# Every third stretch of values made on the chip by GpSimd instead of loaded, in a fused window attention and mixture-of-experts kernel

## The chip, the cores and the metric

The kernel runs on one core of a Trainium2 chip. The metric is the device time of one execution in microseconds (us), lower is better. Engines are called PE (TensorE), DVE (VectorE), ACT (ScalarE), POOL (GpSimd) and SP (SyncE, which issues most of the DMAs here).

## What is computed

There are 8 batches of 8 heads, 512 local and 32 global positions, and a head dimension of 64. Local queries see the global keys and a window of 32 positions to either side; global queries see everything. The result, 4352 tokens of 512 features, goes through a mixture of 8 experts where each token is sent to the one expert with the highest logit.

```python
k_all = concat([k_g, k_l]); v_all = concat([v_g, v_l])
out_g = softmax(q_g @ k_all.T / 8) @ v_all
s_ll = where(abs(pos_i - pos_j) <= 32, q_l @ k_l.T / 8, -1e9)
out_l = softmax(concat([q_l @ k_g.T / 8, s_ll])) @ concat([v_g, v_l])
x = concat([out_g, out_l])                      # 4352 tokens x 512
e = argmax(normed(x) @ normed(expert_emb).T / tau)
out = gate * (relu(x @ w1[e]) @ w2[e])
```

## The kernel before

The work has two stages. The attention stage goes over 8 batches in 4 steps each, 32 steps in all, with 34 slots of program: in slot g the scores of step g are made, the probabilities of step g-1 are turned, and the values of step g-2 are multiplied (the table that `at` fills, lines 843 to 859, and `slot`, line 954). After that the expert stage works on 128-token items with matrix products of 512 columns.

A step treats 4 blocks of 32 queries for 8 heads. Each block of queries needs 128 rows of keys and values: three neighbouring blocks of 32 local rows and the 32 global rows. On the host the values are laid out as 14 such stretches for each batch (`va`, the loop at line 1331): stretch s holds the local blocks s, s+1, s+2, with the global rows in the last place where s is 0, 3, 6, ..., one place earlier where s is 1, 4, ..., and two places earlier where s is 2, 5, .... So stretch 2 reads b2, g, b3, b4 from top to bottom, stretch 0 reads b0, b1, b2, g, and stretch 3 reads b3, b4, b5, g. A stretch is 128 partitions by 260 numbers for each of two groups of heads.

`load_v` (line 290) loads the stretches of one step, 3 or 4 of them by `VCUT` (line 54), for each group: pairs of 260 KB and single ones of 130 KB. `vals` (line 302) says where a stretch stands. `values` (line 529) multiplies them, 64 small matrix products a step. `g_values` (line 616) uses stretches 0, 3, 6, 9, 12 and 13 of a batch for the global queries.

All loads go through SP's queue in the order in which `later` (line 930) lists them for each slot. `deal` and `tick` hand them out evenly over six places in PE's work of that slot, and `paced` (line 262) makes each wait for the PE instruction at that place. Up to 8 loads of this queue are under way at once. The finished token rows leave by indirect DMAs that POOL issues (`send`, line 792; 32 for the local rows), one in each slot from 9 to 28 right after the scores, two in slots 29 and 30.

Of the kernel before, what the change touches and what calls it, by code (L numbers as in the profile page):

```python
# [12 lines left out]
F32 = mybir.dt.float32  # L13
# [12 lines left out]
D = 64  # L26
# [7 lines left out]
P = 128  # L34
# [11 lines left out]
NWIN = NBQ - 2  # L46
VH = D + 1
# [3 lines left out]

GAP = 2
RS = RW + 16
VCUT = (0, 3, 7, 11, NWIN)
VP = 528
VS = 2 * VP
NV = 6
WRUN = 1024
WS = WRUN + GAP

# [13 lines left out]
def _mask_of(i):  # L74
    return 3 if i == 0 else 4 if i == NBQ - 1 else (i - 1) % 3
# [25 lines left out]
def tile_kernel(ctx: ExitStack, tc: tile.TileContext, qk, va, emb, tau, wraw, cst, out):  # L101
    nc = tc.nc
    NB = qk.shape[0]
# [121 lines left out]
    with ExitStack() as actx:  # L225
# [2 lines left out]
        gapi.tile([P, 8], F32, name="gapi_")  # L228
        io = actx.enter_context(tc.tile_pool(name="io", bufs=2))
        vio = actx.enter_context(tc.tile_pool(name="vio", bufs=NV))  # L230
        rt = actx.enter_context(tc.tile_pool(name="rt", bufs=2))
        sp = actx.enter_context(tc.tile_pool(name="sp", bufs=4))
        sm = actx.enter_context(tc.tile_pool(name="sm", bufs=4))
# [9 lines left out]
        NSTEP = 4 * NB  # L243
# [3 lines left out]
        state = {}  # L247
# [4 lines left out]
        def after(ins, mark):  # L252

            tc.add_manual_dep(
                ins.ins,
                mark.ins.name,
                mybir.DependencyInfo(mybir.DependencyClass.Sync, mybir.DependencyReason.DATA),
                reason="pace",
            )
            return ins  # L260

        def paced(ins):

            return after(ins, state["mark"]) if "mark" in state else ins
# [22 lines left out]
            lo, hi = k * RW // 2, (k + 1) * RW // 2  # L287
            paced(nc.sync.dma_start(state["raw", b][:, j, lo:hi], qk[b, :, j * RW + lo : j * RW + hi]))

        def load_v(g, n, m=2):  # L290

            b, s = divmod(g, 4)
            nw = VCUT[s + 1] - VCUT[s]
            if ("v", g) not in state:
                state["v", g] = vio.tile([P, 2, VS], F32, name="vt")
            grp, w = n % 2, n // 2 * m
            for a in range(w, min(w + m, nw), 2):
                n = (min(a + 2, nw) - a) * 4 * VH
                c, to = (VCUT[s] + a) * 4 * VH, a // 2 * VP
                paced(nc.sync.dma_start(state["v", g][:, grp, to : to + n], va[b, grp, :, c : c + n]))  # L300

        def vals(b, w, grp, j):

            s = next(s for s in range(4) if w < VCUT[s + 1])
            n = w - VCUT[s]
            c = n // 2 * VP + (n % 2 * 4 + j) * VH
            return state["v", 4 * b + s][:, grp, c : c + VH]


        first = io.tile([P, 4, RS], F32, name="raw")  # L310
# [10 lines left out]
        def first_step(s):  # L321
            first_part(s * P, (s + 1) * P if s < 3 else QW)
            first_part(QW + KCUT[s] * BQ, QW + KCUT[s + 1] * BQ)
# [3 lines left out]
        for n, i in enumerate((0, NBQ - 2)):  # L327
            for q in range(4):
                m = _mask_of(i + q % 2) * P
                rows = slice(32 * q, 32 * q + 32)  # L330
                nc.gpsimd.tensor_copy(twins[rows, n], mask[rows, m : m + P])
        first_step(1)
        load_v(0, 0, 4)
        load_v(0, 1, 4)
        first_step(2)

        def setup_loads():
# [191 lines left out]
        def values(g):  # L529

            b, s = divmod(g, 4)
            state["o", g] = po = ps_o.tile([P, 2, 512], F32, name="po")
            for grp in range(2):
                pT = state["pT", g, grp]
                for j in range(4):
                    for k in range(4):
                        ins = nc.tensor.matmul(  # L537
                            po[32 * k : 32 * k + 32, grp, j * VH : (j + 1) * VH],
                            pT[:, col(s, k, j) : col(s, k, j) + 32],
                            vals(b, _window(4 * s + k), grp, j),  # L540
                            start=True,
                            stop=True,
                        )
                tick(ins, 4 + grp)
            state["valued"] = ins
# [70 lines left out]
        def g_values(b, grp):  # L616

            og = bank()
            for c, (w, kn) in enumerate(((0, 96), (3, 96), (6, 96), (9, 96), (12, P), (13, P))):
                for j in range(4):  # L620
                    rows = slice(32 * j, 32 * j + 32)
                    nc.tensor.matmul(  # L622
                        og[rows, :VH],
                        gT[:kn, grp, c, rows],
                        vals(b, w, grp, j)[:kn],
                        start=(c == 0),
                        stop=(c == 5),
                    )
            rg = sm.tile([P, 1], F32, name="rg")
            nc.vector.tensor_scalar(rg, og[:, D:VH], 1e-9, None, op0=ALU.add)  # L630
            nc.vector.reciprocal(rg, rg)
            on = sp.tile([P, D], F32, name="on", bufs=2)
            nc.vector.tensor_scalar(on, og[:, :D], rg, None, op0=ALU.mult)
            r0 = 32 * (b % 4)
            xg = state["xg", b // 4][r0 : r0 + 32, 0, grp * 4 * D : (grp + 1) * 4 * D]
            for j in range(4):
                nc.gpsimd.tensor_copy(xg[:, j * D : (j + 1) * D], on[32 * j : 32 * j + 32])
# [191 lines left out]
        for b in range(3, NB - 1, 4):  # L829
            a = b // 4  # L830
# [12 lines left out]
        def at(g, phase, f, *args):  # L843
            plan.setdefault((g, phase), []).append(lambda: f(*args))


        SCORE, TURN, MAX, ACT, VALUE, LOGIT, TAKE, ACT2, GVAL, NORM, BACK, SMALL, LATE, GLOB, SEND = range(15)

        for g in range(NSTEP):
            b, s = divmod(g, 4)  # L850
            at(g, SCORE, scores, g)
            for grp in range(2):
                at(g + 1, TURN, turned, g, grp)
            for grp in range(2):
                at(g, MAX, maxima, g, grp)
                at(g, ACT2 if grp else ACT, exps, g, grp)
                at(g + 1, ACT, take, g, grp)
            at(g + 2, VALUE, values, g)
            at(g + 2, NORM, normed, g)

        for b in range(NB):
            g0 = 4 * b + (0 if b else 2)
# [3 lines left out]
            for part in range(3):  # L866
                g = 4 * b + (2 + part // 2 if b else 4)
# [62 lines left out]
        def later(g, f, *args):  # L930
            loads[g].append(lambda: f(*args))

        for g in range(1, NSTEP):
            for n in range(4):
                later(min(g, NSTEP - 2), load_v, g, n)
        for b in range(1, NB):
            for j in range(4):
                for k in range(2):
                    later(max(4 * b - 5 + j, 0), load, b, j, k)
        for n in range(EARLY + 2):  # L940
            later(4 + n, first_fill, n)

# [6 lines left out]
        for g in loads:  # L949
            n = len(loads[g])  # L950
# [441 lines left out]
```

## Time and profile before

| | us |
|---|---|
| median of 3 runs (lowest, highest) | 726.94 (724.56, 732.45) |
| the profiled execution | 725.47 |
| its span, first to last instruction | 723.6 |

The span ends 1.9 us short of the time of the same execution. Nearly one third of the span is the attention stage, the rest the expert stage. "Idle before, releaser" in a row says how long the engine had nothing to run just before that instruction, and what ended it; "issue" as a releaser means that no semaphore and no other engine is seen to have held it up.

### The profile page before, as it was taken

How to read it: one execution, taken by the hardware profiler on the slowest of the kernel's cores; microseconds unless marked ns; L12 is line 12 of the kernel's file. 1: busy time of each engine (PE TensorE's matmuls, PEld its weight loads, DVE VectorE, ACT ScalarE, POOL GpSimd, SP SyncE). 2: the span in 40 equal slices, each digit the busy share in tenths (PEclk: the TensorE clock that was granted, in tenths of full speed). 3: DMA queues.
4: the chain of work that ended last, by engine and by line, in shares of the span. 5: the costliest groups of instructions: out<-in, count | busy, mean ns of one | idle time of the engine just before them, and what ended most of it. 6: DMA issues, size and time to landing. Idle time of an engine off the chain costs nothing.

```text
span 723.6 us, 23361 instructions
## 1 busy us (share of the span) xinstructions
PE 674.1 (93%) x7867; PEld 535.3 (74%) x7869; DVE 422.2 (58%) x1449; ACT 458.6 (63%) x956; POOL 273.0 (38%) x318
## 2 busy tenths in 40 slices
PE   9888878878878998999999999999999999999996
PEld 4666666656756546888888888888888888888885
DVE  2778777888677763545554554545455545455443
ACT  4776767747767365656565666666666656565664
POOL 2011222222212344545454545444454545454543
PEclk9999999999899999999999999999999999999999
DMA  8988989878997257746565665656565746575654
GB/s 274 351 249 258 256 236 279 285 213 292 283 301 227 77 214 267 260 165 249 186 232 205 209 225 193 244 185 248 169 249 179 259 157 240 185 231 206 223 210 156
DMA packets 66588, 165.13 MB, mean 228 GB/s; under 512 B 6548, under 2 KB 14868, under 8 KB 66464
## 3 DMA queue, kind: packets, MB, share of 16 engines
q1 hardware_dynamic: 60704, 145.67, 60.5%
q0 software_dynamic: 5760, 17.87, 7.0%
q8 instruction: 71, 1.16, 0.7%
q14 instruction: 53, 0.43, 0.2%
HBM read 142.49 MB, written 22.07 MB: 227 GB/s over the span
## 4 chain that ended last, share of the span: by engine, by line
PE 88%; issue 5%; DMA 2%; DVE 2%; SPq 1%; ACT 1%; POOL 0%; DVEq 0%; POOLq 0%
PE g L1198 18%; PE g L1199 18%; PE g L1203 18%; PE po L537 5%; PE hps L1221 4%; PE pt L514 4%; PE s_ps L467 4%; PE pt L654 2%; PE xps L1174 2%; PE pt L622 2%; DMA raw<-in_qk_dram 2%; PE po L355 2%; PE pt L574 1%; PE pt L681 1%; PE s_ps L456 1%
## 5 line engine op out<-in xcount | busy, mean ns | idle before, releaser
L1194 DVE TENSOR_TENSOR WL<-stg,WH 128x512 f32 (+1 forms) x144 | 150.5, 1045 | 130.2 <-ACT WH L1192 130.2
L1194 POOL TENSOR_TENSOR WL<-stg,WH 128x512 f32 (+1 forms) x144 | 174.3, 1210 | 88.9 <-ACT WH L1192 87.9
L1192 ACT CAST WH<-stg 128x512 f32 (+1 forms) x288 | 177.4, 618 | 9.2 <-DMA stg<-in_wraw_dram 4.6
L1198 PE MATMUL g<-WH,hH 128*128 (+1 forms) x288 | 119.5, 415 | 0.0
L1198 PE MATMUL g<-WH,xH 128*128 (+1 forms) x288 | 116.0, 403 | 0.0
L1199 PE MATMUL g<-WL,hH 128*128 (+1 forms) x288 | 113.3, 393 | 0.0
L1203 PE MATMUL g<-WH,xL 128*128 (+1 forms) x288 | 112.6, 391 | 0.0
L1199 PE MATMUL g<-WL,xH 128*128 (+1 forms) x288 | 112.5, 390 | 0.0
L147 POOL DMA_INDIRECT out_dram<-ob x37 | 37.2, 1006 | 151.7 <-ACT ob L145 142.4
L507 ACT ACTIVATE pb<-pb,nm 128x128 f32<-128x128 f32 x256 | 80.1, 396 | 11.7 <-DVE nm L490 11.5
L1203 PE MATMUL g<-WH,hL 128*128 (+1 forms) x288 | 83.4, 391 | 0.0
L1224 DVE TENSOR_TENSOR hL<-hps,hH 128x512 fp32r<-128x512 f32 x72 | 49.8, 692 | 53.8 <-ACT hH L1223 53.6
L1203 PEld LDWEIGHTS g<-WH,hL 128*128 128x128 f32 x288 | 54.1, 188 | 12.1
L1203 PEld LDWEIGHTS g<-WH,xL 128*128 128x128 f32 x288 | 54.1, 188 | 11.6
L145 ACT ACTIVATE ob<-g,xr 128x512 f32<-128x512 f32 x36 | 24.8, 688 | 59.5 <-PE g L1203 59.5
L1199 PEld LDWEIGHTS g<-WL,xH 128*128 128x128 f32 x288 | 54.2, 188 | 10.2 <-DVE ob L146 0.2
L1198 PEld LDWEIGHTS g<-WH,xH 128*128 128x128 f32 x288 | 54.2, 188 | 10.2 <-issue 0.2
L1198 PEld LDWEIGHTS g<-WH,hH 128*128 128x128 f32 x288 | 54.4, 189 | 9.5
L1199 PEld LDWEIGHTS g<-WL,hH 128*128 128x128 f32 x288 | 54.4, 189 | 9.1
L1215 ACT ACTIVATE h<-g 128x512 f32<-128x512 f32 x72 | 42.9, 595 | 28.8 <-PE g L1203 28.8
L794 POOL DMA_INDIRECT xs<-xt,si x32 | 32.1, 1004 | 75.9 <-PE pt L514 27.5
L1223 ACT CAST hH<-hps 128x512 fp32r<-128x512 f32 x72 | 42.0, 584 | 24.6 <-PE hps L1221 24.6
(200 smaller groups left out, 985.4 us busy)
## 6 DMA issues: line engine op xcount, KB each, us to landing
stg<-in_wraw_dram SPq DMA_DIRECT2D x36, 2048.0 KB, 9.8
vt<-in_va_dram SPq DMA_DIRECT2D x96, 260.0 KB, 4.7
raw<-in_qk_dram SPq DMA_DIRECT2D x56, 304.0 KB, 5.1
xr<-xs SPq DMA_DIRECT2D x38, 257.0 KB, 2.7
vt<-in_va_dram SPq DMA_DIRECT2D x32, 130.0 KB, 5.1
stg<-in_wraw_dram SPq DMA_DIRECT2D x16, 256.0 KB, 5.5
xs<-fill SPq DMA_DIRECT2D x12, 257.0 KB, 3.0
stg<-in_wraw_dram SPq DMA_DIRECT2D x4, 512.0 KB, 7.1
```

Of the source, the lines that this page charges most:

```text
L147: nc.gpsimd.indirect_dma_start(out=out[:, :], out_offset=bass.IndirectOffsetOnAxis(ap=ob[:, DM : DM + 1].bitcast(U32), axis=0), in_=ob[:, ...
L507: nc.scalar.activation(pb[:, cs], pb[:, cs], AF.Exp, bias=nm[:, n : n + 1], scale=-1.0)
L537: ins = nc.tensor.matmul(po[32 * k : 32 * k + 32, grp, j * VH : (j + 1) * VH], pT[:, col(s, k, j) : col(s, k, j) + 32], vals(b, _window(4 ...
L794: ins = nc.gpsimd.indirect_dma_start(out=xs[:, :], out_offset=bass.IndirectOffsetOnAxis(ap=st["si"][:, t : t + 1], axis=0), in_=get(t), in ...
L1192: made.append(nc.scalar.copy(WH[:, ds(ra, 1), cs], s3))
L1194: made.append(eng.tensor_tensor(WL[:, ds(r, 1), cs], s3, WH[:, ds(r, 1), cs], ALU.subtract))
L1198: reads.append(nc.tensor.matmul(o.unsqueeze(1), a, WH2[:, ds(rp, 1), sl], start=first, stop=False))
L1199: reads.append(nc.tensor.matmul(o.unsqueeze(1), a, WL2[:, ds(rp, 1), sl], start=False, stop=False))
L1203: reads.append(nc.tensor.matmul(o.unsqueeze(1), a, WH2[:, ds(rp, 1), sl], start=False, stop=last))
L1215: nc.scalar.activation(h[:, nh * 512 : (nh + 1) * 512], g, AF.Relu)
L1223: nc.scalar.copy(hv, hp_)
L1224: nc.vector.tensor_tensor(hL[:, nh * 4 : nh * 4 + 4, :].rearrange("p c n -> p (c n)"), hp_, hv, ALU.subtract)
```

## The change

Only the stretches 0, 1, 3, 4, 6, 7, 9, 10, 12 and 13 of a batch are loaded, as 5 pairs for each group of heads. Stretches 2, 5, 8 and 11 are made in SBUF by `third`: its upper 64 partitions are the lower half of the first stretch of the pair before (b2, g), its lower 64 partitions the upper half of the first stretch of the pair behind (b3, b4). Each is two POOL copies of 64 partitions by 2 x 260 numbers into a new tile `vc` (4 buffers). The loaded pairs have 10 buffers of half the former size in place of 6. `third` of step g stands in slot g+1, the values that need it in slot g+2. The list of loads is cut anew: pairs 0 and 1 of batch b in slot 4b, pairs 2, 3 and 4 in the three slots behind it, and one half load of queries and keys moves one slot later.

```diff
-VCUT = (0, 3, 7, 11, NWIN)
+VW = 4 * VH
+NPAIR = 5
 VP = 528
-VS = 2 * VP
-NV = 6
+VQ = 264
+NV = 10
+NC = 4
...
+        vco = actx.enter_context(tc.tile_pool(name="vco", bufs=NC))
...
-        def load_v(g, n, m=2):
-
-            b, s = divmod(g, 4)
-            nw = VCUT[s + 1] - VCUT[s]
-            if ("v", g) not in state:
-                state["v", g] = vio.tile([P, 2, VS], F32, name="vt")
-            grp, w = n % 2, n // 2 * m
-            for a in range(w, min(w + m, nw), 2):
-                n = (min(a + 2, nw) - a) * 4 * VH
-                c, to = (VCUT[s] + a) * 4 * VH, a // 2 * VP
-                paced(nc.sync.dma_start(state["v", g][:, grp, to : to + n], va[b, grp, :, c : c + n]))
+        def load_v(b, n, grp):
+
+            if ("v", b, n) not in state:
+                state["v", b, n] = vio.tile([P, 2, VP], F32, name="vt")
+            c = n * 3 * VW
+            paced(nc.sync.dma_start(state["v", b, n][:, grp, : 2 * VW], va[b, grp, :, c : c + 2 * VW]))
+
+        def third(b, n):
+
+            t = state["vc", b, n] = vco.tile([P, 2, VQ], F32, name="vc")
+            nc.gpsimd.tensor_copy(t[:D, :, :VW], state["v", b, n][D:, :, :VW])
+            nc.gpsimd.tensor_copy(t[D:, :, :VW], state["v", b, n + 1][:D, :, :VW])
...
+            n, k = divmod(w, 3)
+            if k == 2:
+                return state["vc", b, n][:, grp, j * VH : (j + 1) * VH]
...
-        load_v(0, 0, 4)
-        load_v(0, 1, 4)
+        load_v(0, 0, 0)
+        load_v(0, 0, 1)
...
+            at(g + 1, ACT2, third, b, s)
...
-        for g in range(1, NSTEP):
-            for n in range(4):
-                later(min(g, NSTEP - 2), load_v, g, n)
-        for b in range(1, NB):
-            for j in range(4):
-                for k in range(2):
-                    later(max(4 * b - 5 + j, 0), load, b, j, k)
+        for b in range(NB):
+            for n in range(NPAIR):
+                for grp in range(2):
+                    if b + n:
+                        later(min(4 * b + max(n - 1, 0), NSTEP - 2), load_v, b, n, grp)
+            for i in range(8 if b else 0):
+                later(max(4 * b - 5 + (0, 0, 1, 2, 2, 2, 3, 3)[i], 0), load, b, i // 2, i % 2)
```

SP's queue, before, a run of loads in the middle of the attention stage (`vt` is values, `raw` queries and keys, partitions x numbers):

```order
L300 DMA vt<-in_va_dram 128x520
L300 DMA vt<-in_va_dram 128x260
L300 DMA vt<-in_va_dram 128x520
L288 DMA raw<-in_qk_dram 128x608
L300 DMA vt<-in_va_dram 128x260
L288 DMA raw<-in_qk_dram 128x608
L300 DMA vt<-in_va_dram 128x520 x3
L288 DMA raw<-in_qk_dram 128x608
L300 DMA vt<-in_va_dram 128x520
L288 DMA raw<-in_qk_dram 128x608
L300 DMA vt<-in_va_dram 128x520 x3
```

The same queue of the changed kernel, at about the same place:

```order
L298 DMA vt<-in_va_dram 128x520 x3
L291 DMA raw<-in_qk_dram 128x608
L298 DMA vt<-in_va_dram 128x520 x2
L291 DMA raw<-in_qk_dram 128x608
L298 DMA vt<-in_va_dram 128x520
L291 DMA raw<-in_qk_dram 128x608 x2
L298 DMA vt<-in_va_dram 128x520
L291 DMA raw<-in_qk_dram 128x608
```

The single stretches of 128 x 260 are gone, and so is one third of the pairs: 80 loads of values in the whole kernel where 128 stood.

POOL, before, in the slots in which the rows of batch 0 leave (`xs` is the token rows in DRAM, `xn` the global queries' rows; waits in brackets, DMASW for the landing of a DMA that POOL issued, numbered in turn):

```order
L794 DMA xs<-xt_158,si_161 36992x514 [waits DMAHW3_49,DMAHW2_49,DMAHW4_49,DVE_49,DMAHW5_49,PE_49,Pool_49]
L637 COPY xn_75<-on 32x64 [waits DVE_49]
L637 COPY xn_75<-on 32x64 [waits DMASW0_49]
L637 COPY xn_75<-on 32x64 x2
L794 DMA xs<-xt_158,si_161 36992x514 [waits PE_49,Pool_49]
L794 DMA xs<-xt_158,si_161 36992x514 [waits PE_49]
```

POOL of the changed kernel at the same place:

```order
L799 DMA xs<-xt_159,si_162 36992x514 [waits DMAHW1_49,DMAHW6_49,DVE_49,DMAHW7_49,PE_49,Pool_49]
L303 COPY vc<-vt 64x2x260 [waits DMAHW2_49,DMAHW0_49,DMASW0_49]
L304 COPY vc<-vt 64x2x260 [waits DMAHW4_49,DMAHW1_49]
L642 COPY xn_75<-on 32x64 [waits DVE_49,Pool_49]
L642 COPY xn_75<-on 32x64 [waits Pool_49]
L642 COPY xn_75<-on 32x64 x2
L799 DMA xs<-xt_159,si_162 36992x514 [waits PE_49,Pool_49]
L303 COPY vc<-vt 64x2x260 [waits DMASW1_49]
L304 COPY vc<-vt 64x2x260 [waits DMAHW7_49,DMAHW5_49]
L799 DMA xs<-xt_159,si_162 36992x514 [waits PE_49,Pool_49]
L303 COPY vc<-vt 64x2x260 [waits DMASW2_49]
```

A pair of `vc` copies now stands behind each send. In both programs the copy behind a send waits for that send's landing; before, most sends had another send behind them, and now none has before slot 29, but for one in slot 22.

## Rows read from the trace of the kernel before

**Rows 1.** The page: busy us of each engine; shares of the chain that ended last.

```profile
PE 674.1 (93%) x7867; PEld 535.3 (74%) x7869; DVE 422.2 (58%) x1449; ACT 458.6 (63%) x956; POOL 273.0 (38%) x318
...
PE 88%; issue 5%; DMA 2%; DVE 2%; SPq 1%; ACT 1%; POOL 0%; DVEq 0%; POOLq 0%
```

**Rows 2.** Stretches: length; busy us (instructions) of each engine; granted clock, DMA share, GB/s.

```profile
20.00:240.00 220.00, 180.98 (x5298) 143.30 (x5283) 171.32 (x1025) 149.55 (x403) 43.80 (x99) 0.96 0.84 263
290.00:720.00 430.00, 427.75 (x2085) 353.74 (x2083) 216.88 (x280) 274.07 (x487) 203.03 (x174) 1.00 0.61 212
```

**Rows 3.** PE's waits from 20 to 240 us: us in total, times, longest.

```profile
PE s_ps L467 <- issue: 10.6, 6, 2.4
PE po L537 <- issue: 9.7, 11, 2.0
PE pt L622 <- issue: 6.1, 5, 1.9
PE pt L574 <- issue: 3.4, 2, 1.7
...
PE s_ps L456 <- issue: 1.5, 1, 1.5
PE s_ps L456 <- DMA raw<-in_qk_dram: 1.5, 1, 1.5
```

**Rows 4.** The stretches between the ends of PE's neighbouring "issue" waits, columns as in rows 2.

```profile
54.15:60.40 6.25, 5.24 (x126) 3.96 (x127) 5.19 (x34) 4.18 (x14) 0.00 (x0) 1.00 0.97 291
60.40:64.01 3.61, 3.41 (x127) 2.75 (x127) 2.42 (x16) 3.17 (x10) 0.92 (x4) 1.00 0.77 215
64.01:67.80 3.79, 3.57 (x128) 2.72 (x128) 3.62 (x25) 1.90 (x5) 1.15 (x1) 1.00 0.80 221
67.80:73.45 5.65, 3.39 (x128) 2.59 (x128) 3.62 (x18) 3.88 (x10) 0.23 (x1) 1.00 0.95 257
...
125.23:130.61 5.38, 3.01 (x128) 2.32 (x128) 3.06 (x12) 3.43 (x8) 1.35 (x4) 1.00 0.91 303
...
216.71:220.34 3.63, 3.62 (x128) 3.04 (x128) 2.58 (x19) 2.35 (x5) 2.66 (x5) 1.00 0.46 128
```

**Rows 5.** DMA queues from 20 to 240 us (packets, MB, share of 16 engines), then issues with median landing.

```profile
q1 hardware_dynamic: 28174, 50.36, 75.2%
...
q8 instruction: 42, 0.69, 1.3%
...
vt<-in_va_dram SPq DMA_DIRECT2D x89, 260.0 KB, 4.7
```

**Rows 6.** The same view from 290 to 700 us, in the expert stage.

```profile
out_dram<-ob POOLq DMA_INDIRECT x33, 4.4
```

**Rows 7.** POOL's timeline: start, us, line, what, and [idle before, releaser].

```profile
85.84 0.98 POOL L794 DMA_INDIRECT xs<-xt,si  x1 [4.20 <-PE s_ps L467]
...
94.52 0.99 POOL L794 DMA_INDIRECT xs<-xt,si  x1 [1.88 <-DVE ss L670]
99.27 0.23 POOL L637 COPY xn<-on 32x64 f32<-32x64 f32 x1 [3.76 <-DVE rs L552]
99.87 1.14 POOL L637 COPY xn<-on 32x64 f32<-32x64 f32 x3 [0.37 <-DMA xs<-xt,si]
...
201.84 0.98 POOL L794 DMA_INDIRECT xs<-xt,si  x1 [4.10 <-PE s_ps L467]
207.49 0.23 POOL L637 COPY xg<-on 32x64 f32<-32x64 f32 x1 [4.67 <-DVE rs L552]
208.56 0.78 POOL L637 COPY xg<-on 32x64 f32<-32x64 f32 x3 [0.84 <-DMA xs<-xt,si]
```

**Rows 8.** The sends (line 794): last line of their own view, issue to landing.

```profile
DMA to landing us min/median/max: 3.2/6.0/7.7
```

**Rows 9.** Durations ns min/median/max of copies and two-input operations, by line.

```profile
L637 POOL COPY xn<-on x32: 226/229/717, 42.1 to 129.0; 32x64 f32<-32x64 f32 x32
...
L331 POOL COPY twins<-mask x8: 279/286/292, 6.8 to 9.1; 32x128 f32<-32x128 f32 x8
...
L1194 DVE TENSOR_TENSOR WL<-stg,WH x140: 680/720/2098, 288.3 to 716.3; 128x512 f32 x136, 128x512 fp32r<-128x512 f32 x4
L1194 POOL TENSOR_TENSOR WL<-stg,WH x139: 1088/1282/1418, 290.5 to 713.6; 128x512 f32 x136, 128x512 fp32r<-128x512 f32 x3
...
L1224 DVE TENSOR_TENSOR hL<-hps,hH x72: 678/692/694, 279.5 to 713.9; 128x512 fp32r<-128x512 f32 x72
...
L670 DVE CUSTOM_DVE_ANT_0 junk<-xt x32: 680/683/757, 28.4 to 240.5; 128x512 f32<-128x512 f32 x32
```

**Rows 10.** What SP waits for from 20 to 240 us, the first line.

```profile
SPq L300 <- PE s_ps L467: 40.5, 28, 3.9
```

More of the change, by code (lines that the diff above doesn't have):

```diff
@@ L288, in load @@
             paced(nc.sync.dma_start(state["raw", b][:, j, lo:hi], qk[b, :, j * RW + lo : j * RW + hi]))
-        def load_v(g, n, m=2):
-            b, s = divmod(g, 4)
-            nw = VCUT[s + 1] - VCUT[s]
-            if ("v", g) not in state:
-                state["v", g] = vio.tile([P, 2, VS], F32, name="vt")
-            grp, w = n % 2, n // 2 * m
-            for a in range(w, min(w + m, nw), 2):
-                n = (min(a + 2, nw) - a) * 4 * VH
-                c, to = (VCUT[s] + a) * 4 * VH, a // 2 * VP
-                paced(nc.sync.dma_start(state["v", g][:, grp, to : to + n], va[b, grp, :, c : c + n]))
-        def vals(b, w, grp, j):
[L304 to L307, printed above, removed]
+        def load_v(b, n, grp):
[7 more added lines that the diff above has]
+            nc.gpsimd.tensor_copy(t[D:, :, :VW], state["v", b, n + 1][:D, :, :VW])
+        def vals(b, w, grp, j):
+            n, k = divmod(w, 3)
+            if k == 2:
+                return state["vc", b, n][:, grp, j * VH : (j + 1) * VH]
+            c = k * VW + j * VH
+            return state["v", b, n][:, grp, c : c + VH]
         first = io.tile([P, 4, RS], F32, name="raw")
```

## The prediction

> **What bounds the kernel now.** I read the page first. PE is busy for 93% of the span and makes up 88% of the chain that ended last; waits called "issue" are another 5% [rows 1]. Then the table of stretches. The attention stage, of which 20 to 240 us is the even part, runs 5298 short matrix products and has PE busy for 181 of 220 us; the DMA engines are busy for 0.84 of that time. In the expert stage PE is busy for 428 of 430 us [rows 2]. The change touches only the attention stage, so only there can it win, and at most the 39 us in which PE idles.
>
> PE's waits say whose they are: 10.6 + 9.7 + 6.1 + 3.4 + 1.5 = 31.3 us, in 25 waits, end with no semaphore at all, and a load of queries and keys ends one wait of 1.5 us [rows 3]. PE never waits for a value. The loads do not hold it back in the plain sense: SP itself waits for PE's marks, 40.5 us on one of them alone [rows 10].
>
> So what are these "issue" waits? I cut the timeline where they end. From one end to the next PE runs 126 to 128 matrix products and 127 or 128 weight loads, about 255 instructions each time, whatever the work is [rows 4]. In the same 220 us the instruction queue moves 42 packets of 0.69 MB / 42 = 16.4 KB [rows 5], and 10,581 recorded PE instructions in 42 packets are 252 for each. I read this as PE running dry at the end of a block of instructions whose next block is still on the way through the same DMA engines. What sets the length of the wait stands in the same rows: in stretches with the DMA engines busy for 0.91 to 0.97 of the time PE idles 6.25 - 5.24 = 1.0, then 2.3 and 2.4 us; with 0.46 to 0.80 it idles 0.0 to 0.2 us [rows 4]. The instruction block queues behind data. So the volume of loads costs PE time, though PE waits for none of them.
>
> The Trainium skill (page "Runtime: NRT & Kernel Launch", section "Instruction fetch mechanics") also has blocks of 256 instructions fetched by DMA, but calls the fetch mostly hidden behind the issue of instructions. By that rule fewer loads would give PE nothing. The trace agrees on the block and differs on the hiding: 31.3 us of waits end at block ends.
>
> **What the change does, part by part.** The sum goes against the profiled execution, 725.5 us, which is 1.5 us under the median of the three runs.
>
> *Loads removed.* 128 loads of values become 80: 16 x 260 + 32 x 130 = 8320 KB (8.5 MB) less, 260 KB of them before the start of slot 1. The SP queue moves 50.36 MB in 75.2% of the 220 us [rows 5], so the 8.3 MB that fall here are 12 points of the DMA engines' share: 0.84 becomes 0.72. How much of the 31.3 us goes with it? If the waits fall as the share does, 31.3 x 0.12 / 0.84 = 4.5 us. If nothing is lost below a share of 0.6, as the calm stretches suggest, 31.3 x 0.12 / 0.24 = 15.6 us. I take what a queue gives that fills and empties once in each step, where the mean wait goes with the square of the work: 31.3 x (1 - (0.72 / 0.84)^2) = 8.3 us, that is 0.25 us in each of 32 slots. Bounds: 0 and 15.6.
>
> *Start.* Before the one wait for queries and keys (1.5 us, [rows 3]) 780 KB less of values are in the queue, over 2 us at its rate. The wait goes: -1.5 us. Nothing, at worst.
>
> *Copies on POOL.* 64 copies of 64 x 520 numbers. The trace has copies of 64 numbers at 0.229 us and of 128 at 0.286 us [rows 9], 0.057 us for 64 more; 520 numbers give 0.286 + 0.349 = 0.64 us. Bounds: 0.29 us (if length cost nothing) and 1.28 us (a two-input operation of 512). I take 0.64, the nearest in kind. That is 41 us on an engine that is busy for 44 of 220 us [rows 2], so POOL's busy time binds nothing.
>
> *The wait that comes with them.* POOL's order does bind. In each slot from 9 to 28 a send stands ahead of the two copies, and the first copy waits until that send has landed; the order shown says so, and the trace shows what such a wait is: the send at 94.52 us releases the copies at 99.87, 5.35 us later, the send at 201.84 those at 208.56, 6.7 us later [rows 7]. The median landing is 6.0 us [rows 8]. Before, that cost nothing, since those copies were wanted by nobody for many slots. Now the values of the next slot wait for them. And queued behind the two copies are the four small copies of the global rows (two slots in four, 4 x 0.23 us) and the next send, which then starts late. So POOL now runs a loop. Four slots take 4 x (landing + 0.3 + 2 x 0.64) + 2 x 0.95 + 0.1 us.
>
> PE's own pace is in the same rows: the last sends of batches 0 and 4 stand at 85.84 and 201.84 us [rows 7], sixteen slots apart, 29.0 us for four slots. Without 4 x 0.25 us of instruction waits it is 28.0. The loop at today's landing of 6.0 us is 4 x 7.6 + 2.0 = 32.3 us. But landing gets shorter with a lighter load. The sends of the expert stage, of the same size, land in 4.4 us at a share of 0.61 [rows 2, 6]; between (0.61, 4.4) and (0.84, 6.0) the share of 0.72 gives 5.2 us. The loop is then 4 x 6.8 + 2.0 = 29.1 us. This is the term that I trust least, and it decides. At 29.1 POOL sets the pace in slots 9 to 30, all of the 8.3 us that would fall there are eaten, and 22 / 4 x 0.1 = 0.6 us are lost, which the slack at slot 9 (about a microsecond between the first copies' end and the first use) covers: 0. In slots 29 and 30 two sends each stand in the queue, so the made stretches of slot 30 come one send later: +1.5 us.
>
> *The other 11 slots* have no send ahead of a copy and keep 0.25 us each: -2.7 us. The pairs that `third` reads are issued by the middle of the slot before and land in 4.7 us [rows 5], ahead of it.
>
> *DVE.* In the expert stage an operation of DVE with both inputs in SBUF takes 0.68 to 2.1 us beside POOL's work, one with an input from PSUM 0.68 to 0.69 [rows 9]. In the attention stage only line 670 is of the first kind and wide, 32 times 0.68 us. A slot of 7.25 us has 1.3 us of copies and 0.7 of line 670, so about 9 of 32 meet, at some 0.4 us: 4 us of DVE, which has 49 us idle and 2% of the chain [rows 1, 2]. I take +0.5 us. Bounds: 0, and 9 us if each of the 32 lost 0.3 us on the path.
>
> The Trainium skill (page "SBUF — State Buffer", section "SBUF: two separate sides") states a cause: an exclusive lock on ports that DVE and GpSimd share, held for a whole instruction. The spread in these rows agrees; the sum does not need it.
>
> Sum: -1.5 (start) + 0 (slots 9 to 28) + 1.5 (slots 29, 30) - 2.7 (other slots) + 0.5 (DVE) = -2.2, so 723.3; I say **723.5 us**.
>
> **The rivals.** *Faster, loop hidden.* If sends land in 4.4 us, as in the expert stage, the loop is 4 x 6.0 + 2.0 = 25.9 us, under PE's 28.0. Then the whole gain stays: 725.5 - 8.3 - 1.5 + 0.5 = 716.2 us. For it: landing falls to 3.2 us at best [rows 8]. Against it: the share stays at 0.72.
>
> *Slower, loop unchanged.* If landing stays at 6.0 us (the receipt, not the queue, is what takes long), or a copy takes 1.0 us, the loop is 32.3 to 32.0 us: 22 / 4 x 3.3 = 18, less 1 of slack, plus 1.5 - 2.7 - 1.5 + 0.5: +15, 740.5 us. It decides from a landing of 5.2 us on; each further 0.1 us costs 2.2 us, so that 5.7 us makes the kernel slower by over 1%. PE's waits would then be at line 542, for POOL.
>
> *Loads hidden anyway.* If the block waits are not the load's doing, PE keeps 29.0 us for four slots, the loop's 29.1 hardly shows, and 725.5 - 1.5 + 1.5 + 0.5 = 726.0 us comes out.
>
> **How the numbers follow.** Forecast 0.42, loop hidden 0.25, loop unchanged 0.23, loads hidden 0.10. About 1% is what a measurement of this kernel can tell from no change, 719.7 to 734.2 us around the median. Faster: 0.20 of the hidden loop and 0.03 of the forecast's lower edge, 0.23. Slower: 0.20 of the unchanged loop and 0.03 of its upper edge, 0.23. Same: 0.54. The range reaches from a little under the hidden loop to most of the way to the unchanged one, 714 to 738. The forecast's own range is 719 to 729: a landing of 5.0 to 5.5 us. PE's granted clock, 0.96 on the mean here [rows 2], may move by itself and is within that.
>
> **What would show it.** In the changed profile: (1) a DMA share near 0.72 from 20 to 240 us; (2) "issue" waits near 23 us and none longer at calm stretches; (3) the wait for queries and keys gone; (4) copies of 0.6 to 0.7 us, each pair behind a wait on a send; (5) sends that land in about 5.2 us; (6) some waits of PE at line 542 for POOL, short and in slots 9 to 31; (7) line 670 a little longer at worst. The forecast is wrong if landing does not follow the load, if the copies are far from 0.64 us, or if the block waits do not follow the share.

## The result, and the profile after

The changed kernel is slower: 739.16 us (median of 6 executions, 737.49 to 741.73) against 726.92 us (6 executions, 724.56 to 732.45). The ratio is 1.0145, with a 95% interval of 1.0108 to 1.0182. The forecast was 723.5 us with a range of 714 to 738; it missed, and it named slower by over 1% with a chance of 0.23.

The profiled execution of the changed kernel took 741.73 us, 16.3 us more than that of the kernel before. First its page, busy time of each engine and the chain that ended last:

```profile
PE 680.2 (92%) x7867; PEld 537.8 (73%) x7869; DVE 428.4 (58%) x1449; ACT 459.0 (62%) x956; POOL 314.6 (43%) x382
...
PE 75%; DVE 8%; issue 7%; DMA 4%; POOL 3%; ACT 1%; SPq 1%; POOLq 0%; DVEq 0%
```

Against [rows 1], PE's part of the chain falls from 88% to 75%; DVE, DMA and POOL, 4% together before, have 15%. Next the stretch from 20 to 240 us (columns as in [rows 2]) and the larger of PE's waits from 20 to 255 us (us in total, times, longest):

```profile
20.00:240.00 220.00, 174.34 (x4984) 136.20 (x4985) 168.69 (x982) 142.87 (x386) 77.23 (x145) 0.96 0.74 220
```

```profile
PE po L542 <- POOL vc L304: 18.8, 11, 4.5
PE s_ps L472 <- issue: 7.6, 5, 3.4
PE po L542 <- issue: 5.9, 12, 0.9
...
PE pt L627 <- issue: 2.4, 5, 0.5
...
PE s_ps L461 <- issue: 0.9, 2, 0.6
```

The DMA share fell from 0.84 to 0.74, the "issue" waits from 31.3 us [rows 3] to 17.2 (with one of 0.4 us that is not shown), and the wait for queries and keys is gone. In their place stands a wait that the kernel before did not have: 18.8 us at line 542 for the second copy of a made stretch. POOL's timeline (start, us, line, what, [idle before, releaser]) says why it is late:

```profile
66.24 1.16 POOL L799 DMA_INDIRECT xs<-xt,si  x1 [2.43 <-PE pt L519]
...
88.80 1.32 POOL L799 DMA_INDIRECT xs<-xt,si  x1 [0.65 <-PE po L542]
...
105.00 1.00 POOL L799 DMA_INDIRECT xs<-xt,si  x1 [0.28 <-POOL xn L642]
110.49 0.61 POOL L303 COPY vc<-vt 64x520 f32<-64x520 f32 x1 [4.49 <-DMA xs<-xt,si]
111.16 0.61 POOL L304 COPY vc<-vt 64x520 f32<-64x520 f32 x1
111.93 0.99 POOL L799 DMA_INDIRECT xs<-xt,si  x1 [0.16 <-POOL vc L304]
116.17 0.61 POOL L303 COPY vc<-vt 64x520 f32<-64x520 f32 x1 [3.24 <-DMA xs<-xt,si]
116.84 0.62 POOL L304 COPY vc<-vt 64x520 f32<-64x520 f32 x1
117.52 0.10 POOL L730 MEMSET ohb<- 128x8 bf16 x1
118.27 1.00 POOL L799 DMA_INDIRECT xs<-xt,si  x1 [0.65 <-PE pt L519]
...
213.81 1.00 POOL L799 DMA_INDIRECT xs<-xt,si  x1 [0.65 <-PE po L542]
```

In each slot the send comes first, its landing releases the copies, and the next send comes behind them: 105.00, 111.93, 118.27 us. The copies and the landing are near what the forecast said, 0.64 and 5.2 us (durations ns min/median/max, and issue to landing from 60 to 250 us):

```profile
L304 POOL COPY vc<-vt x31: 612/617/1042, 22.6 to 245.3; 64x520 f32<-64x520 f32 x31
...
DMA to landing us min/median/max: 4.0/5.3/6.9
```

For the split of the 16.3 us two more rows are needed, POOL's send of slot 9 and PE's first product of the expert stage, in the kernel before:

```profile
66.36 1.15 POOL L794 DMA_INDIRECT xs<-xt,si  x1 [2.43 <-PE pt L514]
```

```profile
268.75 0.60 PE L1174 MATMUL xps<-ident,xr 128*128 128x128 f32 x4
```

and of the changed kernel:

```profile
283.77 0.60 PE L1180 MATMUL xps<-ident,xr 128*128 128x128 f32 x4
```

| stretch | before, us | after, us | difference | forecast by its own terms |
|---|---|---|---|---|
| to the send of slot 9 | 66.36 | 66.24 | -0.1 | -1.5 - 8 x 0.25 = -3.5 |
| to the send of slot 28 [rows 7] | 135.48 | 147.57 | +12.1 | 0 |
| to the expert stage's first product | 66.91 | 69.96 | +3.0 | +1.5 - 3 x 0.25 = +0.7 |
| to the end of the span | 454.9 | 456.1 | +1.3 | 0 |

Three quarters of the loss lie where every slot has a send ahead of its copies. The attention stage is 268.75 of 723.6 us in the kernel before, 37% of the span, a little more than the third named above.

### The profile page after: what moved, and what is told of

Same layout as the page of the kernel before. It is cut to its first block, busy times and chain, and to the rows that moved or that the text cites. A ratio compares the mean times of both kernels' runs of the same rounds, so it can differ in the third digit from the quotient of the medians.

```text
span 739.9 us, 23380 instructions
## 1 busy us (share of the span) xinstructions
PE 680.2 (92%) x7867; PEld 537.8 (73%) x7869; DVE 428.4 (58%) x1449; ACT 459.0 (62%) x956; POOL 314.6 (43%) x382
## 4 chain that ended last, share of the span: by engine, by line
PE 75%; DVE 8%; issue 7%; DMA 4%; POOL 3%; ACT 1%; SPq 1%; POOLq 0%; DVEq 0%
PE g L1204 18%; PE g L1205 18%; PE g L1209 17%; PE hps L1227 4%; PE po L542 4%; PE xps L1180 2%; DMA stg<-in_wraw_dram 2%; PE pt L519 2%; PE s_ps L472 2%; DVE pb L495 1%; PE pt L659 1%; POOL vc L304 1%; PE pt L686 1%; PE pt L180 1%; DMA vt<-in_va_dram 1%
## 5 line engine op out<-in xcount | busy, mean ns | idle before, releaser
L1209 PEld LDWEIGHTS g<-WH,hL 128*128 128x128 f32 x288 | 54.1, 188 | 12.1
L303 POOL COPY vc<-vt 64x520 f32<-64x520 f32 x32 | 19.8, 617 | 99.3 <-DMA xs<-xt,si 75.8
L542 PE MATMUL po<-vc,pT 128*32 128x65 f32 x512 | 42.2, 234 | 21.1 <-POOL vc L304 18.8
```

Of the source, the lines that this page charges most:

```text
L542: ins = nc.tensor.matmul(po[32 * k : 32 * k + 32, grp, j * VH : (j + 1) * VH], pT[:, col(s, k, j) : col(s, k, j) + 32], vals(b, _window(4 ...
L1209: reads.append(nc.tensor.matmul(o.unsqueeze(1), a, WH2[:, ds(rp, 1), sl], start=False, stop=last))
```

## The experiments

Single executions of the kernel before ranged from 718 to 732 us on the chips used here. So times below are medians with the ratio's interval against executions of the kernel before in between, and a profile is read for what waits for what; its single times carry some of that spread too. "Expert stage at" is the start of PE's first product of that stage in the profiled execution.

| kernel | median us (n) | ratio to before, 95% | issue waits, PE for POOL, 20 to 240 us | expert stage at |
|---|---|---|---|---|
| before | 725.4 to 727.8 | 1 | 31.5, 0 | 268.75 |
| changed | 739.16 (6) | 1.0145 [1.0108, 1.0182] | 17.2, 18.8 | 283.77 |
| copies left out | 729.35 (10) | 1.004 [0.9996, 1.0083] | 23.1, 0 | 262.19 |
| thirds loaded | 725.45 (10) | 0.9987 [0.9943, 1.0032] | 32.1, 0 | 275.72 |
| idle copies | 737.60 (4) | 1.018 [1.0086, 1.0275] | 18.4, 14.5 | 280.41 |
| idle copies, fill on DVE | 736.02 (4) | 1.0157 [1.008, 1.0234] | 26.6, 0 | 280.58 |
| copies ahead of the send | 727.02 (10) | 1.0003 [0.9958, 1.0048] | 15.2, 6.8 | 268.00 |
| copies a slot early | 731.66 (10) | 1.0071 [1.0041, 1.0102] | 21.7, 12.9 | 275.74 |
| rows on ACT | 724.75 (10) | 0.997 [0.994, 1.0] | 13.9, 13.6 | 272.23 |
| sends together | 737.79 (4) | 1.0177 [1.012, 1.0234] | 5.7, 26.9 | 280.95 |
| copies on ACT | 725.82 (10) | 0.9971 [0.993, 1.0011] | 21.4, 0 | 273.87 |
| ahead, sends together | 724.40 (10) | 0.9955 [0.9925, 0.9986] | 13.2, 9.5 | 267.95 |
| ahead, sends by twos | 720.54 (10) | 0.9921 [0.9887, 0.9954] | 14.9, 10.4 | 265.44 |
| ahead, twos apart | 723.72 (12) | 0.9972 [0.9939, 1.0006] | 17.3, 2.5 | 263.19 |

(Waits are summed over all lines.) The theory behind the first runs: POOL's loop of send, landing and copies took the gain of the loads and more. The rivals: the loads gave nothing, or the copies cost time by themselves.

### What fewer loads give

**Copies left out.** Stretch 3n+2 is read from the first stretch of its pair, so the attention output is another one.

```diff
             if k == 2:
-                return state["vc", b, n][:, grp, j * VH : (j + 1) * VH]
+                k = 0
...
-            at(g + 1, ACT2, third, b, s)
```

> The changed kernel with the copies left out: every third stretch is read from the first stretch of its pair instead (the attention output is therefore another; loads, matrix products and sends are those of the changed kernel). It shows what fewer loads give alone. Theory (instruction blocks wait behind data): issue waits about 17 us from 20 to 240 us instead of 31, no raw wait, 711 to 718 us. Rival (loads were hidden anyway): 725 to 728 us.

The stretch from 20 to 240 us and the longest of PE's waits from 20 to 255 us:

```profile
20.00:240.00 220.00, 187.99 (x5328) 145.67 (x5308) 173.88 (x1043) 151.86 (x408) 46.60 (x102) 0.95 0.74 229
```

```profile
PE s_ps L472 <- issue: 10.1, 5, 3.1
PE po L542 <- issue: 4.6, 7, 1.7
```

The time of 729 us looks as if the loads had been hidden. It is not so: the expert stage begins 6.6 us earlier than before, but it has more to do, because other attention outputs are sent to other experts and the number of items that the stage works on depends on that. The expert stage of this kernel, and of the kernel before (columns as in [rows 2]):

```profile
263.90:720.60 456.70, 455.56 (x2218) 376.50 (x2217) 229.53 (x297) 291.41 (x518) 216.01 (x185) 1.00 0.62 216
```

```profile
270.50:716.70 446.20, 443.27 (x2159) 366.49 (x2158) 224.15 (x289) 283.41 (x504) 210.53 (x180) 1.00 0.62 216
```

PE works 12.3 us longer there, on 59 more matrix products in the trace. So the loads are worth about 6.6 us of the attention stage in this profile, and the issue waits are 23.1 us at a share of 0.74. The time itself decides nothing. PE's pace shows it too. It turns the probabilities in slots 12 and 28 at

```profile
83.80 1.09 PE L519 MATMUL pt<-ident,pb 128*128 128x128 f32 x8
...
195.29 1.09 PE L519 MATMUL pt<-ident,pb 128*128 128x128 f32 x8
```

which is (195.29 - 83.80) / 4 = 27.9 us for four slots, against 29.0 before ([rows 7]; the sends there follow PE).

**Thirds loaded.** The tile of the copies is filled by two DMAs of 130 KB: the old volume in the new order.

```diff
+            if n < 4:
+                if ("vc", b, n) not in state:
+                    state["vc", b, n] = vco.tile([P, 2, VQ], F32, name="vc")
+                paced(nc.sync.dma_start(state["vc", b, n][:, grp, :VW], va[b, grp, :, c + 2 * VW : c + 3 * VW]))
...
-            at(g + 1, ACT2, third, b, s)
```

> The changed kernel with every third stretch loaded by its own two DMAs of 130 KB into the tile that the copies filled, and no copies: the volume of loads of the kernel before, in the pairs and nearly in the order of the changed kernel. Theory (volume): the DMA share is back at 0.84, issue waits back near 31 us, 724 to 731 us. Rival (the order and the size of the loads made the issue waits shorter, not the volume): share 0.84, but issue waits near 17 us, 712 to 719 us.

```profile
PE s_ps L476 <- issue: 12.5, 6, 3.5
PE po L546 <- issue: 12.1, 9, 4.1
```

The share is 0.85, and the issue waits are 32.1 us. It is the volume that makes them (64 loads more than without copies), not the order of the pairs. This profiled execution took 731.2 us, 5.8 more than the median, so its stage boundary is not compared; PE's pace in it, from the same two slots, is that of the kernel before, (205.70 - 89.56) / 4 = 29.0 us:

```profile
89.56 1.09 PE L523 MATMUL pt<-ident,pb 128*128 128x128 f32 x8
...
205.70 1.09 PE L523 MATMUL pt<-ident,pb 128*128 128x128 f32 x8
```

### What the copies cost

**Idle copies.** The kernel before, all loads kept, with the same 64 copies at the same places into a tile that nobody reads.

```diff
+        def third(g):
+            t = vco.tile([P, 2, VQ], F32, name="vc")
+            v = state["v", g]
+            nc.gpsimd.tensor_copy(t[:D, :, :VW], v[D:, :, :VW])
+            nc.gpsimd.tensor_copy(t[D:, :, :VW], v[:D, :, :VW])
...
+            at(g + 1, ACT2, third, g)
```

> The kernel before, with all its loads, plus the 64 copies of 64 x 520 numbers at the places on POOL that they have in the changed kernel, into a tile that nobody reads. Theory (the copies cost only through the wait of the values for them): 726 to 729 us, sends later by up to 1.3 us a slot with nobody waiting. Rival (the copies slow DVE, or delay the sends so that a buffer of tokens comes free late): 732 us or more, with longer operations of DVE or waits of PE for DVE.

It is 1.8% slower, against what I expected: no value waits for POOL, and PE still waits 19.3 us for it from 20 to 255 us.

```profile
PE pt L767 <- POOL ohb L735: 19.3, 6, 4.8
```

`ohb` is a fill of 128 x 8 numbers of 0.10 us that the routing of each batch needs. It stands on POOL behind the copies, and a batch's routing on PE now gets it late, six times.

**Idle copies, fill on DVE.** The same with that fill moved, so that nothing that PE uses soon is left on POOL.

```diff
-                nc.gpsimd.memset(ohb[:, nt], 0.0)
+                nc.vector.memset(ohb[:, nt], 0.0)
```

> The kernel before with the copies that nobody reads, as in the run that took 737.6 us, but with the small fill of the one-hot tile, for which PE waited 19.3 us there, on DVE instead of POOL. Theory (the copies cost only what is queued behind them on POOL and waited for): PE's waits for POOL gone, 726 to 730 us. Rival (the copies cost by themselves, through DVE): 734 us or more.

PE's waits for POOL are gone, and the time stays. PE's waits from 20 to 275 us, and POOL's sends of slots 12 and 28:

```profile
PE pt L164 <- DMA raw<-xs: 7.5, 1, 7.5
```

```profile
94.22 1.00 POOL L804 DMA_INDIRECT xs<-xt,si  x1 [0.15 <-POOL vc L310]
...
215.31 0.99 POOL L804 DMA_INDIRECT xs<-xt,si  x1 [0.15 <-POOL vc L310]
```

Here POOL goes at its own pace, hardly held up by another engine: (215.31 - 94.22) / 4 = 30.3 us for four slots, where the kernel before takes 29.0 [rows 7]. It falls behind slot by slot, and at the end PE waits 7.5 us for token rows that were sent late. PE's turning in slot 32, in this kernel and in the kernel before, shows that the bill comes at the end:

```profile
231.67 1.36 PE L524 MATMUL pt<-ident,pb 128*128 128x128 f32 x8
```

```profile
228.69 1.27 PE L514 MATMUL pt<-ident,pb 128*128 128x128 f32 x8
```

PE is 3.0 us late there and 11.8 us late at the expert stage. That is the cleanest measurement of the loop: it is longer than PE's four slots, and the bill comes wherever PE next needs something from POOL. My expectation of 726 to 730 us was wrong for that reason. The time is in the rival's range, 734 us or more, but a cost of the copies by themselves, through DVE or otherwise, would have to lie in the 3.0 us.

### What in POOL's loop does it

**Copies ahead of the send.**

```diff
-            at(g + 1, ACT2, third, b, s)
+            at(g + 1, SEND, third, b, s)
```

> The changed kernel, with the two copies of a slot put ahead of that slot's send on POOL instead of behind it, so that they wait for the send of the slot before, which left a slot earlier. Theory (POOL's loop of send, landing, copies): PE's waits at line 542 for POOL, 18.8 us in the changed kernel, fall below 3 us, and with them the half-speed stretches of PE that follow them; the issue waits stay near 17 us; 739 - 19 - 3 = 717 us, 712 to 721. Rival (the copies themselves cost: DVE slowed beside POOL, PE's small waits for ACT and DVE): those stay, 727 to 735 us. Rival (landing of the paired loads holds the copies): waits at 542 stay above 10 us, 730 us or more.

```profile
PE po L542 <- POOL vc L304: 6.8, 6, 2.3
```

The copies now wait for the landing of a send that left a slot earlier, and the changed kernel loses its loss: 727.0 us. The waits of PE for POOL are 6.8 us, not under 3; the time is above what the theory said and at the edge of the rival on the copies' own cost. POOL still waits for a landing in every slot, but the fill, the gap behind it and the first of the small row copies now lie inside that wait.

**Copies a slot early**, behind the same send, with the loads a slot earlier and one more buffer.

```diff
-NC = 4
+NC = 5
...
-            at(g + 1, ACT2, third, b, s)
+            at(max(g, 1), ACT2, third, b, s)
...
-                        later(min(4 * b + max(n - 1, 0), NSTEP - 2), load_v, b, n, grp)
+                        later(min(max(4 * b + max(n - 2, -1), 0), NSTEP - 2), load_v, b, n, grp)
```

> The changed kernel with each pair of copies one slot earlier (and the loads of its pairs one slot earlier, one more buffer for what is made), still behind the send of its slot. POOL's loop of send, landing, copies is the same, but the values come one slot, about 7 us, later than the copies. Theory (the loop's mean fits into PE's pace; the gain went because single slots are late and nothing wins them back): PE's waits for POOL fall from 18.8 us to under 5, 716 to 724 us. Rival (POOL's mean pace is the limit, 31 us for four slots with or without slack): waits stay above 10 us, 730 us or more.

```profile
PE pt L762 <- POOL ohb L730: 10.9, 5, 4.2
...
PE po L542 <- POOL vc L304: 2.0, 1, 2.0
```

A slot of slack takes the wait of the values away, 18.8 to 2.0 us, and the fill becomes the next thing that PE waits for. The rival was right here: with slack or without, POOL's mean pace is too long. The sends of slots 12 and 28 stand at 94.04 and 214.43 us, 30.1 us for four slots. The end of one round of the loop in this kernel:

```profile
122.40 0.10 POOL L730 MEMSET ohb<- 128x8 bf16 x1
123.16 1.00 POOL L799 DMA_INDIRECT xs<-xt,si  x1 [0.65 <-DMA vt<-in_va_dram]
```

Between fill and send POOL idles 0.65 us, whatever is named as the releaser; the same 0.65 us stand there in the changed kernel at 88.80, 118.27 and 213.81 us (0.23 us once, at 156.89 us).

**Rows on ACT.** The copies of the global rows, in two slots of four, leave POOL.

```diff
-                nc.gpsimd.tensor_copy(xg[:, j * D : (j + 1) * D], on[32 * j : 32 * j + 32])
+                nc.scalar.copy(xg[:, j * D : (j + 1) * D], on[32 * j : 32 * j + 32])
```

> The changed kernel with the small copies of the global rows (line 642, four of 0.26 us and 0.28 us of idle time, in two slots of four) on ACT instead of POOL. Those are the two slots whose loop took 8.1 to 8.8 us against 6.3 to 6.9 in the others. Theory (the two long slots are late): with 6.8 us in all four slots, under PE's 7.0 to 7.25, the waits for POOL fall to under 9 us, 724 to 731 us. Rival (the send and its landing alone set it): waits above 14 us, 735 us or more.

```profile
PE po L542 <- POOL vc L304: 13.6, 12, 5.3
```

724.75 us is in the theory's range, 1.75 points of the ratio or some 13 us under the changed kernel, for 2 x 1.33 = 2.7 us less of POOL in four slots. The sends of slots 12 and 28 stand at 87.22 and 203.35 us: four slots take 29.0 us instead of 31.25. The waits for POOL fell less than I said, to 13.6 us, but one of them, 5.3 us at 227.41 us, stands behind the two sends of slots 29 and 30 and not in the loop of one send a slot; without it they are 8.3 us. The waits account for 5.2 us of the 13; what the rest is no run separates.

**Sends together.** The four sends of a batch at the end of one slot, behind its copies.

```diff
-                    at(g0 + 6 + t, SEND, r.send, t, "scored")
+                    at(g0 + 7, LATE, r.send, t, "valued")
```

> The changed kernel with the four sends of a batch (batches 0 to 4) issued one behind the other at the end of one slot in four, behind that slot's copies, instead of one in each slot ahead of the copies. Copies and loads stay. POOL then waits for one landing in four slots: 4 x 1.3 + 5.3 + 4 x 1.3 + 2.1 = 18 us of 28. Theory (loop): PE's waits for POOL fall from 18.8 us to under 5, 718 to 726 us. Rival (the copies slow DVE or their loads land late): waits elsewhere stay, 730 us or more. Rival (four sends at once crowd the DMA engines): issue waits above 25 us, 728 us or more.

```profile
PE po L542 <- POOL vc L304: 26.9, 8, 4.8
```

A miss: POOL's work in four slots is short now, but the copies of the next slot wait for the last of four landings, and PE waits 3.8 to 4.8 us for them once in each of the five batches. Sends issued together also land later, at a median of 6.5 us against 5.3 (6.9 with four sends at once and the copies ahead). It is not only the mean of the loop that counts; a single late slot costs PE its whole wait.

### Other places for the work

**Copies on ACT** (`nc.scalar.copy` in `third`).

> The changed kernel with the 64 copies on ACT instead of POOL, at the same places. POOL's order is then that of the kernel before and no value waits for a send. Theory (POOL's loop took the gain of the loads and more): no waits of PE for POOL; the attention stage ends near the 264 us that the kernel without copies showed (270.5 before, 285.5 in the changed kernel), plus what about 64 x 0.6 = 38 us more work on ACT costs PE, 0 to 6 us: 717 to 726 us. Rival (half of the copies' harm is not POOL's order): 730 us or more.

No wait for POOL is left, and 725.8 us comes out, the upper end of what was expected. PE now waits for ACT (this profiled execution took 729.7 us, 3.9 more than the median):

```profile
PE pt L519 <- ACT xT L666: 9.6, 11, 2.1
```

**Ahead, sends together**: both edits, the sends in phase SEND of one slot.

> Both at once: copies ahead of the sends in a slot, and the four sends of a batch together in one slot of four, near its beginning. Theory (loop): no wait of PE for POOL is left, 715 to 722 us, under the kernel before. Rival (copies slow DVE, which PE then waits for): 723 to 728 us.

**Ahead, sends by twos:**

```diff
-            at(g + 1, ACT2, third, b, s)
+            at(g + 1, SEND, third, b, s)
...
-                    at(g0 + 6 + t, SEND, r.send, t, "scored")
+                    at(g0 + 7 + t // 2, SEND, r.send, t, "scored")
```

> The changed kernel with the copies ahead of the sends in their slot, and the sends of a batch by twos in two slots of four (those without copies of global rows). POOL waits for two landings in four slots instead of four, and no slot for more than 6.6 us. Theory (loop): PE's waits for POOL, 6.8 us with the copies ahead alone and 9.5 us with four sends in one slot, fall under 3 us, 717 to 722 us, under the kernel before by 0.7% or more. Rival (copies slow DVE and PE follows): 723 to 727 us.

**Ahead, twos apart**: `g0 + 6 + t // 2 * 2` in the same place.

> As with the sends by twos, but the two slots with sends lie apart (the first and the third of the four slots in which a batch was sent), so that the landing of one pair is over a slot before the next pair is issued. With the pairs in neighbouring slots PE still waited 10.4 us for POOL, two thirds of it where one pair's landing delayed the next pair or the copies behind it. Theory (what makes POOL late is landings in a row without slack): PE's waits for POOL under 6 us, the rest of them where the last batches send, 716 to 721 us. Rival (what is left comes from the copies' loads or from DVE): waits and time as with neighbouring pairs, 719 to 724 us.

With four sends at once PE still waits 9.5 us for POOL, where I had said none: 6.3 us of it where the copies of the slot behind wait for the last of four landings, as above, and 3.2 us in the last slots, where batch 5 sends two in a slot. Two of the three are faster than the kernel before beyond their intervals: by 0.45% with four sends at once, by 0.79% with sends by twos, 720.5 us. For the pairs in neighbouring slots the time is as expected, but not for the reason given, since PE's waits for POOL did not fall under 3 us:

```profile
PE po L542 <- POOL vc L304: 10.4, 6, 2.7
```

With the pairs apart they did:

```profile
PE po L542 <- POOL vc L304: 2.5, 1, 2.5
```

and its profiled execution, 718.8 us, begins the expert stage at 263.19 us, but that execution is the fastest of 12: the median is 723.7 us, in the rival's range, and its interval reaches over 1. The two were timed beside different executions of the kernel before, and which of them is better stays open. What the sends by twos in neighbouring slots show is that a part of the loads' gain can be had when POOL is less in the way.

## Why the prediction was wrong, point by point

**What bounds the kernel: right.** Issue waits follow the volume of loads: 31.5 and 32.1 us at shares of 0.84 and 0.85, 23.1 at 0.74 without copies. The forecast's price, by the square of the share, was 31.3 - 8.3 = 23.0 us; that it is met to a tenth is luck, since other kernels in which PE does not wait for POOL have 26.6 us at 0.84 (idle copies, fill on DVE) and 21.4 at 0.75 (copies on ACT). PE's pace without the third stretches, 27.9 us for four slots, is the forecast's 28.0. In the changed kernel the issue waits are even 17.2 us. Part of them probably falls into times when PE waits for POOL anyway: with idle copies, at a share of 0.83, they are 18.4 us beside 14.5 us of waits for POOL.

**Start and loads: near, then lost.** The wait at the start went. Without copies the expert stage begins 6.6 us earlier; the forecast had 1.5 + 8.3 = 9.8. In the changed kernel nothing of it is left by slot 9 (-0.1 us), although no send stands ahead of a copy there. Without copies the send of slot 9 is at 63.89 us, 2.5 us earlier than before. What ate these 2.4 us stays open, and much of it may be the spread of single executions: the kernel with the sends together runs the same program up to slot 9 and turns the probabilities there at 63.38 us, against 65.17 in the changed kernel, 65.01 before and 62.83 without copies. The changed kernel's trace has PE waiting 1.0 and 0.9 us for two operations of DVE and 1.9 us for one of ACT in that time.

**Copies: right.** A median of 0.62 us against 0.64.

**Landing: right number, wrong reason.** Medians are 5.3 us in the changed kernel against the forecast 5.2. But with all loads they are 5.4 (thirds loaded) and 5.3 us (idle copies), at shares of 0.85 and 0.83, and 5.4 without the third stretches at 0.74 (all from 60 to 225 us). So landing does not follow the load as I drew it through [rows 6, 8]; the 6.0 us of one profile carried that line, and the number came out by luck.

**POOL's loop: the step that failed.** "The loop is then 4 x 6.8 + 2.0 = 29.1 us" was 30.3 us when POOL ran alone and 30.1 with a slot of slack. The landing and the copies in it were right; small things were left out. Four slots of the changed kernel, from its timeline: gaps of 0.16 to 0.28 us ahead of the sends, and 0.65 us behind the fill, where I had put 0.3 each; 1.10 instead of 0.95 us for each group of four row copies; the send of global rows in slot 22, named in the order and not priced, 1.3 us in 16 slots; and copies stretched to about 1 us, four in 16 slots. Together about 1.2 us for four slots, 5 us in 16: 29.1 becomes 30.3.

The second half of the same step was the sentence that POOL "sets the pace" at its own mean. From slot 12 to slot 28 the changed kernel took (213.81 - 88.80) / 4 = 31.25 us for four slots. PE waited for POOL in some slots; in others POOL waited for DVE or PE, as in these two rows of the changed kernel:

```profile
164.26 1.04 POOL L642 COPY xg<-on 32x64 f32<-32x64 f32 x4 [2.03 <-DVE on L638]
166.78 1.00 POOL L799 DMA_INDIRECT xs<-xt,si  x1 [1.48 <-PE pt L519]
```

Two engines that wait for each other in turn take in each slot the longer of the two, and a mean over four slots hides that. This half is read from the trace and was not tried alone. What the step cost in all is 4 x (31.25 - 29.0) = 9.0 us from slot 12 to 28, and 3.1 more from slot 9 to 12, where the forecast had 0.

**The slack: too small to matter.** About a microsecond at slot 9 was to cover a loss of 0.6 us; the loss was 12.1 us.

**Slots 29 and 30: right in place, short in size.** The wait behind two sends was 4.5 us, where the forecast had +1.5: the copies start at 237.33 us, 5.4 us after the second send ends. PE's clock was at half behind it (below).

**DVE: mis-sized.** The forecast looked at line 670, wide and of two inputs from SBUF, which stays at a median of 0.68 us. It is the short operations that suffer. A chain of 27 of them, 128 x 4 numbers with two inputs from SBUF, before and after (ns min/median/max):

```profile
L390 DVE SCALAR_TENSOR_TENSOR nwa<-nwa,ss x27: 159/163/167, 51.0 to 243.1; 128x4 f32<-128x4 f32 x21, 128x1 f32<-128x1 f32 x3, 128x5 f32<-128x5 f32 x3
```

```profile
L395 DVE SCALAR_TENSOR_TENSOR nwa<-nwa,ss x27: 159/164/611, 51.6 to 258.3; 128x4 f32<-128x4 f32 x21, 128x1 f32<-128x1 f32 x3, 128x5 f32<-128x5 f32 x3
```

Up to the expert stage DVE is busy for 203.5 us instead of 196.1 with the same 1159 instructions; line 670 has 0.3 us of these 7.4. The Trainium skill (page "SBUF — State Buffer", section "SBUF: two separate sides") says that the loser of the port that DVE and GpSimd share waits for a whole instruction. The trace agrees: the longest lost about 611 - 163 = 448 ns, which is within one copy of 617. With the same copies on ACT, DVE is busy for 196.0 us, so it is POOL's copies that lengthen its work. On the path they cost little: in the kernel in which POOL is hardly waited for (twos apart) PE takes 27.7 us for four slots between slots 12 and 28, 27.9 without copies.

**The rivals.** "Slower, loop unchanged", 740.5 us, is what came: PE waits at line 542 for POOL. Its condition, a landing of 6.0 us or copies of 1.0, did not; the loop was long at a landing of 5.3, so that its number was met is luck in part. Its chance of 0.23 was too small, since a loop priced at 29.1 against PE's 29.0 left no room for a term forgotten, and each 0.1 us was priced at 2.2. "Loads hidden anyway" is refuted by the issue waits and PE's pace with and without the third stretches.

## What to carry to other kernels

An engine that is busy for a third of the time can still set the pace when its queue holds a wait in every round: write its round out instruction by instruction from the timeline, gaps included, before comparing it with the round of the engine that needs it. Where two rounds come out equal, expect the slower of the two in each round, not their mean, and put the awaited work ahead of the instruction whose landing holds up the queue, and then, if need be, issue such instructions by twos so that fewer rounds wait; groups of four without the first step did not help (737.8 us). And look at what else stands in that queue behind the new work: PE waited 19.3 us for a fill of 0.1 us here, as long as for the values themselves, and when the fill was moved away it waited for the next thing from POOL.

## What the runs showed of the hardware that was not expected

Behind its long waits PE worked at half its clock. With the sends together PE waited 4.42 us until 115.43 us; the wait, and the stretch with its end and the one behind it (columns as in [rows 2]; the last three are granted clock, DMA share, GB/s):

```profile
115.43 0.31 PE L542 MATMUL po<-vc,pT 128*32 128x65 f32 x1 [4.42 <-POOL vc L304]
```

```profile
112.00:116.00 4.00, 0.57 (x24) 0.57 (x28) 1.24 (x12) 3.28 (x10) 1.73 (x4) 0.74 0.58 181
116.00:120.00 4.00, 4.00 (x115) 3.75 (x115) 1.05 (x6) 0.23 (x1) 1.17 (x4) 0.50 0.50 125
```

From 116 to 120 us the clock is at the lower of its two levels, 1.2 GHz, just when PE has work again. The five waits of 3.8 to 4.8 us in that kernel are all followed by 4 us at a clock of 0.50 to 0.58, and the 7.5 us with idle copies and the fill on DVE by 4 us at 0.50. The changed kernel shows the same after the wait of 4.5 us that ends at 238.66 us: a clock of 0.50 from 240 to 244 us, with PE busy throughout. Shorter waits show both, so the length of a wait is not all that decides: in the changed kernel one of 3.4 us until 74.88 us is followed by 4 us at 1.00, one of 1.9 us until 35.70 us by 4 us at 0.57. So these waits cost more than their length; by an estimate from the row of 240 to 244 us (0.50, PE busy for 4.00 us), up to (1 - 0.50) x 4 = 2 us more.
